# DeltaNet and soft MoE on one core: unscaled keys, block transposes on VectorE, and 24 chunk slots with work eight chunks ahead

## The chip, the core and the metric

The kernel runs on one core of one Trainium2 chip. Five engines of that core work side by side, each through its own instructions in order: TensorE (PE in the profile, its weight loads PEld), VectorE (DVE), ScalarE (ACT), GpSimd (POOL) and SyncE (SP), which here only issues DMAs. TensorE reads SBUF and writes PSUM; the other engines move results back. The metric is the device time of one execution in microseconds (us), lower is better.

## The reference

An attention block with the delta rule feeds a mixture of experts with soft slots. Four batches times eight heads are 32 independent sequences of 768 tokens with head size 48; everything is float32.

```python
k_n = k / (np.linalg.norm(k, axis=-1, keepdims=True) + 1e-06)
for t in range(S):
    kt, vt, bt = (k_n[:, :, t], v[:, :, t], beta[:, :, t, None])
    y[:, :, t] = np.einsum('bhd,bhde->bhe', q[:, :, t], state)
    v_old = np.einsum('bhde,bhd->bhe', state, kt)
    state = state + bt[:, :, :, None] * np.einsum('bhd,bhe->bhde', kt, vt - v_old)
...
logits = x @ phi                                  # x: (3072, 384), 32 slots
d = softmax of logits over the 3072 tokens
slot_input = d.T @ x
slot_out = per expert e: relu(slot_input[e] @ w1[e]) @ w2[e]
c = softmax of logits over the 32 slots
return c @ slot_out
```

`x` is the attention output, with the eight heads of a token side by side.

## The kernel before, in words

**Chunks and groups.** The 768 tokens are cut into 24 chunks of 32. Within a chunk the recurrence is solved as a triangular system, so that only the state S (48x48 for each of the 32 sequences) passes from chunk to chunk. Four chunks are a group; there are six groups. On the 128 partitions lie four heads (index `h`) times 32 tokens; the other eight of the 32 (batch, head) pairs (`U = 8`) lie side by side on the free axis.

**Norms (L155 to L180), per group.** POOL squares the keys (L163), DVE adds them up (L164) and takes the root with one correction step (L168 to L174, the square root itself on ACT), and POOL multiplies the keys by the reciprocal (L177).

**Preparation of a chunk (`prep`, L182).** TensorE transposes K and Q (L193), ACT copies the result to KQ (L196), TensorE multiplies K with K and with Q (L208); ACT copies the K-K products to `Lc` (L212) and DVE masks the others into `AT` with `tri` (L213). `pt`, the PSUM tile of these steps and of the routing, has two buffers, so TensorE cannot be more than two tiles ahead of the copies.

**Inversion of a group (`invert`, L218).** The 128 triangular systems of a group (32 sequences times four chunks) are inverted at once, one system per partition. For that `Lc` has to be regrouped: four DMAs write it to DRAM (`ld`, L228), one reads it back (`lb`, L229), and POOL multiplies by beta (L230). Then come 31 eliminations of two DVE operations each (L242 and L245). POOL multiplies by beta again (L249), a DMA writes the inverse to DRAM (`td`, L252), and per chunk four DMAs bring its part back (`TT`, L262).

**A chunk (`chunk`, L272)** is a chain: psR (L282), R = V - psR on DVE (L287), psW with the inverse (L293), U on DVE (L296), psS (L303), then the state S, half copied by ACT (L315) and half by DVE (L313), and the next chunk's psR needs S. psY (L282 and L320) and its copy Y (L322) hang beside the chain.

**Routing of a group (`route`, L330)**: transposes of Y (L340), logits (L349), both softmaxes with a running maximum, and the sums over tokens (L414).

**After the six groups** come the experts (L553, L577) and the output (L603 to L610). Two of the eight w1 are loaded early, the other weights once the attention's buffers are free.

**Order.** The kernel hands out steps: `Fill` puts a quarter of a slot's steps between the stages of a chunk, `merge` interleaves lists. In group n the first two chunks carry the preparation of group n+1, the last two its inversion and the routing of group n-1. The Tile framework then fixes each engine's order; every instruction waits in its place on its engine.

Of the kernel before, what the change touches and what calls it, by code (L numbers as in the profile page):

```python
# [16 lines left out]
def kernel(  # L17
# [20 lines left out]

    nc = tc.nc
    P = 128  # L40
# [19 lines left out]
    dp = ctx.enter_context(tc.tile_pool(name="dp", bufs=2, space=bass.MemoryType.DRAM))  # L60
# [14 lines left out]
    def load(src, dst, n, eng):  # L75
        for c in range(GC):
            for h in range(4):
                s0 = (n * GC + c) * C
                eng.dma_start(
                    out=dst[C * h:C * h + C, c, :, 0:D],  # L80
                    in_=src.rearrange("b (g h) s d -> h s (b g) d", h=4)[h, s0:s0 + C])

    def load_k(n, eng=nc.sync):
        load(k, Ks[n % 3], n, eng)

    def load_q(n, eng=nc.sync):
        load(q, Qs, n, eng)

    def load_v(n, eng=nc.sync):
        Vt[n] = io.tile([P, GC, U, D], F32, name="V", tag="V")  # L90
        load(v, Vt[n], n, eng)

    for t in Ks + [Qs]:
        nc.gpsimd.memset(t[:, :, :, D:DP], 0.0)

    bb = cpool.tile([P, NG, C], F32, name="bb")
    load_k(0)
    load_q(0, nc.scalar)
    for h in range(4):
        for c in range(GC):  # L100
            p0 = C * h + U * c
            nc.scalar.dma_start(
                out=bb[p0:p0 + U],
                in_=beta.rearrange("b (g h) (n c t) -> h c (b g) n t", h=4, c=GC, t=C)[h, c])
    load_v(0)
    phi = cpool.tile([GD, 4, NSL], F32, name="phi")
    for g in range(G):
        nc.scalar.dma_start(
            out=phi[g * D:(g + 1) * D],
            in_=moe_phi[g * 4 * D:(g + 1) * 4 * D].rearrange("(h d) s -> d h s", h=4))  # L110


    ident = cpool.tile([P, P], F32, name="ident")
    make_identity(nc, ident)
# [15 lines left out]
    TTs = [wk.tile([P, U, C], F32, name=f"TT{i}", bufs=1) for i in range(2)]  # L130
# [22 lines left out]
    KQ, AT, Lc, TTb = {}, {}, {}, {}  # L153

    def norm(n):  # L155
        Kf = Ks[n % 3].rearrange("p c u d -> p (c u) d")
        ssq = small.tile([P, GC * U], F32, name="ssq", tag="ssq")
        nrm = small.tile([P, GC * U], F32, name="nrm", tag="nrm")
        rn = small.tile([P, GC * U], F32, name="rn", tag="rn")

        def squares():
            sq = wk.tile([P, GC * U, D], F32, name="sq", tag="sq", bufs=1)
            nc.gpsimd.tensor_tensor(sq, Kf[:, :, 0:D], Kf[:, :, 0:D], op=ALU.mult)  # L163
            nc.vector.tensor_reduce(ssq, sq, axis=AX.X, op=ALU.add)  # L164

        def root():

            nc.vector.tensor_scalar(ssq, ssq, 1e-30, None, op0=ALU.max)  # L168
            nc.scalar.activation(nrm, ssq, ACT.Sqrt)
            nc.vector.reciprocal(rn, nrm)  # L170
            nc.vector.tensor_tensor(rn, rn, ssq, op=ALU.mult)
            nc.vector.tensor_tensor(nrm, nrm, rn, op=ALU.add)
            nc.vector.tensor_scalar(nrm, nrm, 0.5, 1e-6, op0=ALU.mult, op1=ALU.add)
            nc.vector.reciprocal(rn, nrm)  # L174

        def scale():
            nc.gpsimd.tensor_tensor(Kf[:, :, 0:D], Kf[:, :, 0:D],  # L177
                                    rn.unsqueeze(2).broadcast_to([P, GC * U, D]), op=ALU.mult)

        return [squares, root, scale]  # L180

    def prep(n, c):  # L182

        cc = n * GC + c

        def transposes(bh):
            if bh == 0:
                KQ[cc] = wk.tile([P, B, 2, P], F32, name="KQ", tag="KQ", bufs=2 * GC - 1)
            tp = pt([P, 2, 2, P])
            for i in range(2):  # L190
                b = 2 * bh + i
                for a, src in enumerate((Ks[n % 3], Qs)):
                    nc.tensor.transpose(  # L193
                        tp[:, i, a, :],
                        src[:, c, b * G:(b + 1) * G, :].rearrange("p g d -> p (g d)"), ident)
            nc.scalar.activation(KQ[cc][:, 2 * bh:2 * bh + 2], tp, ACT.Copy)  # L196

        def products():
            AT[cc] = wk.tile([P, G, B, C], F32, name="AT", tag="AT", bufs=2 * GC - 1)
            if c == 0:  # L200
                Lc[n] = wk.tile([P, GC, B, G, C], F32, name="Lc", tag="Lc", bufs=1)
            pg = [pt([P, B, 2, C]) for _ in range(G)]
            for b in range(B):
                for h in range(4):
                    for g in range(G):
# [4 lines left out]
                                         start=True, stop=True, skip_group_check=True)  # L210
            for g in range(G):
                nc.scalar.activation(Lc[n][:, c, :, g, :], pg[g][:, :, 0, :], ACT.Copy)  # L212
# [5 lines left out]
    def invert(n):  # L218
# [3 lines left out]
        def spread():  # L222
            lb = st["lb"] = wk.tile([P, C, C], F32, name="lb", tag="lb", bufs=1)
            lc = Lc.pop(n).rearrange("p c b g t -> p (c b g) t")
            ld = dp.tile([P, C, C], F32, name="ld", tag="ld")
            for h in range(4):
# [3 lines left out]
            nc.gpsimd.tensor_tensor(lb, lb, bb[:, n].unsqueeze(2).broadcast_to([P, C, C]),  # L230
                                    op=ALU.mult)
# [4 lines left out]

# [402 lines left out]
```

## Time and profile before

| | us |
|---|---|
| runs (three) | 605.12, 606.75, 613.19; median 606.75 |
| profiled execution, its own time | 610.76 |
| its span (first to last instruction) | 609.0 |
| PE busy | 333.6 (55% of the span) |
| DVE busy | 253.1 (42%) |
| ACT busy | 113.5 (19%) |
| POOL busy | 71.2 (12%) |
| mean granted TensorE clock | 0.698 of full speed |

The time lies 1.76 us above the span: what passes before the first and after the last instruction. PEclk is the clock that TensorE was granted, 1.00 being full speed. In a row of the windows view stand the stretch, its length, then busy time and count of PE, PEld, DVE, ACT and POOL, then PEclk, the share of the DMA engines and GB/s. In a row of the groups view stand line, engine, operation, tiles, shape and count, then busy time in all and mean ns of one, then the idle time of the engine before them and what ended it. In a row of the waits view: who waited for whom, us in all, times, the longest. In the timeline: start, length, what.

### The profile page before, as it was taken

What the parts mean: (1) busy time and instruction counts of PE and PEld (TensorE: products, weight loads), DVE (VectorE), ACT (ScalarE), POOL (GpSimd) and SP (SyncE); (2) the same over time, 40 slices, a digit from 0 to 9 for tenths busy, and PEclk for the clock granted to TensorE, in tenths of its full rate; (3) what the DMA queues carried; (4) which work ended last, traced back from release to release, by engine and by line L of the source; (5) the groups of instructions that cost most, each with busy time, mean ns of one, the idle gap of its engine ahead of it and who ended that gap; (6) DMA issues with size and microseconds to landing.
All of it is one profiled execution on the core that took longest, in us unless ns stands there. A gap on an engine that the chain in (4) does not pass through costs nothing.

```text
span 609.0 us, 20685 instructions
## 1 busy us (share of the span) xinstructions
PE 333.6 (55%) x9387; PEld 252.6 (41%) x9387; DVE 253.1 (42%) x661; ACT 113.5 (19%) x232; POOL 71.2 (12%) x62
## 2 busy tenths in 40 slices
PE   0360274550189730697702877405987528769675
PEld 0250153540167520576601665304766417553224
DVE  2214951129812369223297123693246722130013
ACT  0230130110033310223200323102343001211003
POOL 4203110011210110400303001103001010000000
PEclk9995556675557975568755588855689565869975
DMA  6406017562034510235300445102230024497918
GB/s 118 80 15 133 8 37 216 110 119 46 1 85 79 118 29 0 67 67 111 62 0 6 83 74 114 30 0 58 35 74 3 1 55 119 177 427 278 430 42 311
DMA packets 138296, 58.12 MB, mean 95 GB/s; under 512 B 131552, under 2 KB 134624, under 8 KB 136160
## 3 DMA queue, kind: packets, MB, share of 16 engines
q1 hardware_dynamic: 132544, 55.87, 34.6%
q10 hardware_dynamic: 5664, 0.94, 0.9%
q8 instruction: 73, 1.20, 0.8%
q14 instruction: 15, 0.12, 0.1%
HBM read 45.76 MB, written 11.01 MB: 93 GB/s over the span
## 4 chain that ended last, share of the span: by engine, by line
PE 44%; DVE 26%; DMA 12%; issue 5%; ACT 5%; SPq 4%; POOL 3%; ACTq 0%; DVEq 0%
DVE pr L242 9%; DVE tt L245 9%; PE pt L193 7%; PE psW L293 5%; PE pt L208 4%; PE pt L414 4%; PE psR L282 4%; PE psY L320 3%; PE psS L303 3%; DMA w2t<-in_moe_w_dram 3%; PE psY L282 3%; PE pt L340 3%; PE pso L577 2%; DMA TT<-td 2%; DMA Qs<-in_q_dram 2%
## 5 line engine op out<-in xcount | busy, mean ns | idle before, releaser
L193 PE MATMUL pt<-ident,Ks 128*128 128x128 f32 x96 | 40.4, 422 | 172.4 <-POOL Ks L177 137.5
L193 PEld LDWEIGHTS pt<-ident,Ks 128*128 128x128 f32 x96 | 20.1, 210 | 177.8 <-POOL Ks L177 163.6
L242 DVE TENSOR_TENSOR pr<-tt,lb 128x31 f32<-128x31 f32 (+15 forms) x186 | 78.0, 419 | 18.5 <-POOL lb L230 13.4
L245 DVE TENSOR_TENSOR tt<-tt,pr 128x31 f32<-128x31 f32 (+15 forms) x186 | 65.9, 355 | 5.5
L293 PE MATMUL psW<-R,TT 32*32 32x48 f32 x1536 | 37.5, 232 | 27.1 <-DMA TT<-td 25.1
L208 PE MATMUL pt<-KQ 48*32 48x64 f32 x1536 | 41.5, 287 | 6.0 <-issue 4.1
L293 PEld LDWEIGHTS psW<-R,TT 32*32 32x32 f32 x1536 | 29.4, 126 | 36.9 <-DMA TT<-td 19.6
L296 DVE COPY U<-psW 128x384 f32<-128x384 f32 x24 | 13.4, 557 | 74.9 <-PE psW L293 74.9
L196 ACT ACTIVATE KQ<-pt 128x512 f32<-128x512 f32 x48 | 28.4, 597 | 78.7 <-PE pt L193 78.7
L313 DVE COPY S<-psS 48x768 f32<-48x768 f32 x23 | 22.1, 960 | 46.0 <-ACT S L315 46.0
L193 PE MATMUL pt<-ident,Qs 128*128 128x128 f32 x96 | 38.8, 407 | 0.0
L315 ACT ACTIVATE S<-psS 48x768 f32<-48x768 f32 x23 | 18.5, 804 | 103.6 <-PE psS L303 103.2
L282 PE MATMUL psR<-S,KQ 128*32 128x96 f32 x768 | 31.8, 303 | 8.5 <-DVE S L313 6.0
L213 DVE TENSOR_TENSOR AT<-pt,tri 128x128 f32<-128x128 f32 x48 | 12.0, 286 | 58.6 <-ACT Lc L212 58.6
L208 PEld LDWEIGHTS pt<-KQ 48*32 48x32 f32 x1536 | 28.8, 140 | 18.1 <-ACT KQ L196 10.1
L320 PE MATMUL psY<-U,AT 32*32 32x48 f32 x1536 | 29.4, 233 | 4.9 <-issue 4.1
L177 POOL TENSOR_TENSOR Ks<-Ks,rn 128x1536 f32<-128x1536 f32 x6 | 16.6, 2770 | 123.7 <-DVE pr L242 88.8
L282 PE MATMUL psY<-S,KQ 128*32 128x96 f32 x768 | 29.9, 297 | 1.7 <-issue 1.7
L282 PEld LDWEIGHTS psR<-S,KQ 128*32 128x32 f32 x768 | 23.4, 135 | 14.4 <-DVE S L313 7.9
L303 PE MATMUL psS<-U,Ks 32*48 32x48 f32 x1472 | 22.7, 242 | 11.3 <-DVE U L296 8.7
L414 PE MATMUL pt<-Y,dr 32*32 32x97 f32 x768 | 26.1, 308 | 4.0 <-ACT dr L407 4.0
L320 PEld LDWEIGHTS psY<-U,AT 32*32 32x32 f32 x1536 | 24.7, 128 | 8.1 <-issue 5.9
(118 smaller groups left out, 438.8 us busy)
## 6 DMA issues: line engine op xcount, KB each, us to landing
w1t<-in_moe_w_dram SPq DMA_DIRECT2D x8, 1536.0 KB
w2t<-in_moe_w_dram SPq DMA_DIRECT2D x8, 1536.0 KB
Ks<-in_k_dram SPq DMA_DIRECT2D x96, 48.0 KB
V<-in_v_dram SPq DMA_DIRECT2D x96, 48.0 KB
out_dram<-ob SPq DMA_DIRECT2D x24, 192.0 KB
Qs<-in_q_dram SPq DMA_DIRECT2D x80, 48.0 KB
ld<-Lc SPq DMA_DIRECT2D x24, 128.0 KB
lb<-ld SPq DMA_DIRECT2D x6, 512.0 KB
```

Of the source, the lines that this page charges most:

```text
L193: nc.tensor.transpose(tp[:, i, a, :], src[:, c, b * G:(b + 1) * G, :].rearrange("p g d -> p (g d)"), ident)
L196: nc.scalar.activation(KQ[cc][:, 2 * bh:2 * bh + 2], tp, ACT.Copy)
L208: nc.tensor.matmul(pg[g][rh, b], lhsT=KQ[cc][r, b, 0, rh], rhs=KQ[cc][r, b, :, rh], start=True, stop=True, skip_group_check=True)
L242: nc.vector.tensor_tensor(prv, tt[:, 0:m, j:j + 1].broadcast_to([P, m, w]), lb[:, j, j + 1:C].unsqueeze(1).broadcast_to([P, m, w]), op=ALU ...
L245: nc.vector.tensor_tensor(tt[:, 0:m, j + 1:C], tt[:, 0:m, j + 1:C], prv, op=ALU.subtract)
L282: nc.tensor.matmul(dst[hs[h], b].rearrange("p g d -> p (g d)"), lhsT=kq[:, b, a, hs[h]], rhs=old[:, h, b, :], start=(b == 0), stop=False, ...
L293: nc.tensor.matmul(pw[hs[h], u], lhsT=T[hs[h], u], rhs=R[hs[h], u], start=(u == 0), stop=True, skip_group_check=True)
L303: nc.tensor.matmul(psS[DP * g:DP * g + D, h, b * D:(b + 1) * D], lhsT=K[hs[h], c, b * G + g, 0:D], rhs=Ut[hs[h], b * G + g], start=(cc == ...
L313: nc.vector.tensor_copy(dst, src)
L315: nc.scalar.activation(dst, src, ACT.Copy)
L320: nc.tensor.matmul(py[hs[h], b, g], lhsT=at[hs[h], g, b], rhs=Ut[hs[h], b * G + g], start=False, stop=True, skip_group_check=True)
L414: nc.tensor.matmul(pa[r], lhsT=st["dr"][r, c, b, :], rhs=Yn[r, c, b, 0:GD + 1], start=(b == 0), stop=(b == B - 1), skip_group_check=True)
```

## The change

**Unscaled keys.** The norm of a key now comes from the diagonal of the K-K products (`norms`), so the steps on whole key tiles are gone (squares, their sum, the scaling). With nm the norm plus 1e-6, the weight of a token becomes `gm` = beta / nm^2, and V is multiplied by nm (`scale_v`, one POOL operation of 128x384 per chunk); keys stay as loaded.

**Transposes on DVE.** `Lc` is written so that a 32x32 block transpose on DVE regroups it (`spread`); after the eliminations, which now run over the rows of `tt`, a second one turns the inverse back (`back`). The DRAM tiles and their DMAs are gone. U is copied by ACT instead of DVE, with two buffers, as has R.

**24 slots.** Loads are per chunk. A slot x runs chunk x, prepares chunk x+8, does a quarter of the inversion of the next group and a quarter of the last group's routing, loads K and Q twelve ahead and V six ahead. Slots -8 to -1 have no chunk. Beta and phi are loaded from POOL instead of ACT.

```diff
-    Ks = [io.tile([P, GC, U, DP], F32, name=f"Ks{i}", bufs=1) for i in range(3)]
-    Qs = io.tile([P, GC, U, DP], F32, name="Qs", bufs=1)
+    LEAD, AHEAD = 8, 12
+    NK, NQ = AHEAD + 1, AHEAD - LEAD + 1
+    Ks = [io.tile([P, U, DP], F32, name=f"K{i}", bufs=1) for i in range(NK)]
+    Qs = [io.tile([P, U, DP], F32, name=f"Q{i}", bufs=1) for i in range(NQ)]
...
     for h in range(4):
         for c in range(GC):
             p0 = C * h + U * c
-            nc.scalar.dma_start(
+            nc.gpsimd.dma_start(
                 out=bb[p0:p0 + U],
...
-    def norm(n):
...
-            nc.gpsimd.tensor_tensor(sq, Kf[:, :, 0:D], Kf[:, :, 0:D], op=ALU.mult)
-            nc.vector.tensor_reduce(ssq, sq, axis=AX.X, op=ALU.add)
...
-            nc.gpsimd.tensor_tensor(Kf[:, :, 0:D], Kf[:, :, 0:D],
-                                    rn.unsqueeze(2).broadcast_to([P, GC * U, D]), op=ALU.mult)
...
+            by = Lc[n].rearrange("p t (c b g) -> p c g b t", c=GC, b=B)
             for g in range(G):
-                nc.scalar.activation(Lc[n][:, c, :, g, :], pg[g][:, :, 0, :], ACT.Copy)
+                nc.scalar.activation(by[:, c, g], pg[g][:, :, 0, :], ACT.Copy)
...
         def spread():
             lb = st["lb"] = wk.tile([P, C, C], F32, name="lb", tag="lb", bufs=1)
-            for h in range(4):
-                r = slice(C * h, C * h + C)
-                nc.sync.dma_start(out=ld[r].rearrange("u s t -> s u t"), in_=lc[r])
-            nc.sync.dma_start(out=lb, in_=ld)
-            nc.gpsimd.tensor_tensor(lb, lb, bb[:, n].unsqueeze(2).broadcast_to([P, C, C]),
-                                    op=ALU.mult)
+            nc.vector.transpose(lb.rearrange("p t s -> p (t s)"),
+                                Lc.pop(n).rearrange("p t c -> p (t c)"))
...
+        def norms():
...
+            dg = st["lb"].rearrange("p t s -> p (t s)")[:, 0:C * C:C + 1]
+            nc.vector.tensor_scalar(ssq, dg, 1e-30, None, op0=ALU.max)
+            nc.scalar.activation(nrm, ssq, ACT.Sqrt)
...
+            nc.vector.tensor_tensor(gm, rn, rn, op=ALU.mult)
+            nc.vector.tensor_tensor(gm, gm, bb[:, n], op=ALU.mult)
+            nc.gpsimd.tensor_tensor(st["lb"], st["lb"],
+                                    gm.unsqueeze(2).broadcast_to([P, C, C]), op=ALU.mult)
+            nT[n] = small.tile([P, C], F32, name="nT", tag="nT")
+            nc.vector.transpose(nT[n], nrm)
...
-            TTb[n] = dp.tile([P, C, C], F32, name="td", tag="td")
-            nc.sync.dma_start(out=TTb[n], in_=st["tt"])
+        def back():
+            TT[n] = wk.tile([P, C, C], F32, name="TT", tag="TT")
+            nc.vector.transpose(TT[n].rearrange("p c i -> p i c"), st["tt"])
...
+    def scale_v(cc):
         n, c = divmod(cc, GC)
+        nc.gpsimd.tensor_tensor(
+            Vt[cc], Vt[cc], nT[n][:, c * U:(c + 1) * U].unsqueeze(2).broadcast_to([P, U, D]),
+            op=ALU.mult)
...
-        nc.vector.tensor_copy(Ut, pw)
+        nc.scalar.activation(Ut, pw, ACT.Copy)
...
+    for x in range(-LEAD, NCH):
+        n, c = divmod(x, GC)
+        if x + AHEAD < NCH:
+            load_k(x + AHEAD)
+            load_q(x + AHEAD)
+        if 0 <= x + 6 < NCH:
+            load_v(x + 6)
...
+        if c == 0:
+            inv = invert(n + 1) if 0 <= n + 1 < NG else []
+        if 0 <= x + 2 < NCH:
+            scale_v(x + 2)
+        steps = merge(prep(x + LEAD) if x + LEAD < NCH else [], quarter(inv, c),
+                      quarter(routing, c))
+        if x < 0:
+            drain(steps)
+            continue
+        fill = Fill(steps)
+        chunk(x, Ys[n % 2], fill)
+        fill(last=True)
+        if c == GC - 1:
+            routing = route(n, Ys[n % 2])
```

**Place one: POOL at the start.** Before, after the pads of the key tiles, POOL prepares `bdm`, from which DVE makes the mask `tri`:

```order
L94 MEMSET Ks_78 128x32x16
L94 MEMSET Ks_79 128x32x16
L94 MEMSET Ks_80 128x32x16
L94 MEMSET Qs 128x32x16
masks.py:197 MEMSET ident 128x128
L116 MEMSET hm 128x4
L123 MEMSET bdm 128x128
masks.py:199 ISA
masks.py:199 AFFINE_SELECT ident<-ident 128x128
L117 AFFINE_SELECT hm<-hm 128x4
L124 AFFINE_SELECT bdm<-bdm 128x128
```

Now, on the same engine:

```order
masks.py:197 MEMSET ident 128x128
L113 DMA bb<-in_beta_dram 8x6x32
masks.py:199 ISA
masks.py:199 AFFINE_SELECT ident<-ident 128x128
L113 DMA bb<-in_beta_dram 8x6x32 x15
L118 DMA phi<-in_moe_phi_dram 48x4x32 x2
L124 MEMSET hm 128x4
L131 MEMSET bdm 128x128
L125 AFFINE_SELECT hm<-hm 128x4
```

The 18 DMAs of beta and phi stand on POOL ahead of `bdm`, and so ahead of the first mask that DVE applies.

**Place two: PE in a loaded slot.** Before, from the second to the third chunk of the second group, with routing beside it:

```order
L303 MATMUL psS<-U,Ks_79 48x48 x32
L320 MATMUL psY<-U,AT 32x48 x32
L340 MATMUL pt<-ident,Y_581 96x128 x5
L282 MATMUL psR<-S_173,KQ 32x96 x16
L282 MATMUL psY<-S_173,KQ 32x96 x16
L293 MATMUL psW<-R,TT_170 32x48 x32
```

Now, in chunk 10 of 0 to 23 (K_79 holds the keys of chunk 16, which is prepared meanwhile):

```order
L278 MATMUL psR<-S_180,KQ 32x96 x16
L278 MATMUL psY<-S_180,KQ 32x96 x13
L173 MATMUL pt<-ident,Q_90 128x128
L173 MATMUL pt<-ident,K_79 128x128
L173 MATMUL pt<-ident,Q_90 128x128 x2
L173 MATMUL pt<-ident,K_79 128x128
L173 MATMUL pt<-ident,Q_90 128x128
L278 MATMUL psY<-S_180,KQ 32x96 x3
L336 MATMUL pt<-ident,Y_188 96x128 x4
L188 MATMUL pt<-KQ 32x64 x32
L336 MATMUL pt<-ident,Y_188 96x128 x4
L289 MATMUL psW<-R,TT 32x48 x32
```

Between psR and psW there now stand six of the eight transposes and all products of another chunk.

**Place three: DVE in the same slot.** Before, the eliminations of a group end in one block and the chunk's own operations follow:

```order
L242 TENSOR_TENSOR pr<-tt,lb 128x31
L245 TENSOR_TENSOR tt<-tt,pr 128x31
L213 TENSOR_TENSOR AT<-pt,tri 128x128 x6
L296 COPY U<-psW 128x384
L313 COPY S_175<-psS 48x16x48
L287 TENSOR_TENSOR R<-V,psR 128x384
```

Now, around the R of the same slot:

```order
L243 TENSOR_TENSOR tt<-tt,pr 128x21x11
L195 TENSOR_TENSOR AT<-pt,tri 128x128 x2
L240 TENSOR_TENSOR pr<-tt,lb 128x240
L243 TENSOR_TENSOR tt<-tt,pr 128x20x12
L240 TENSOR_TENSOR pr<-tt,lb 128x247
L283 TENSOR_TENSOR R<-V,psR 128x384
L243 TENSOR_TENSOR tt<-tt,pr 128x19x13
```

R stands behind the masks AT of the prepared chunk and behind three eliminations; in the whole list the 62 operations of an inversion lie almost wholly in two of a group's four slots, with AT, R and S strewn among them.

More of the change, by code (lines that the diff above doesn't have):

```diff
@@ L128 @@
     nc.vector.tensor_reduce(tri, bdm.rearrange("p h t -> p t h"), axis=AX.X, op=ALU.add)
-    TTs = [wk.tile([P, U, C], F32, name=f"TT{i}", bufs=1) for i in range(2)]
     psS = psp.tile([P, 4, 512], F32, name="psS")
@@ L149, in load_w2, with prep @@
         nc.sync.dma_start(out=w2t[e], in_=moe_w2[e].rearrange("(p t) d -> p t d", t=NFC))
[L153 to L184 removed]
+    KQ, AT, Lc, TT, nT = {}, {}, {}, {}, {}
+    def prep(cc):
+        n, c = divmod(cc, GC)
         def transposes(bh):
             if bh == 0:
[L188 removed]
+                KQ[cc] = wk.tile([P, B, 2, P], F32, name="KQ", tag="KQ", bufs=LEAD + 1)
             tp = pt([P, 2, 2, P])
```

140 lines of the change are left out of this document (58 added, 82 removed).

## The prediction

> **What bounds the kernel now.** I read the busy time by stretches first, with borders at the first transposes of each group (POOL's scaled keys release them), then who waits for whom, then the chain. Columns of the stretches: PE, PEld, DVE, ACT, POOL busy (instructions), granted clock, DMA share, GB/s.
>
> ```profile
> 161.60:244.20 82.60, 46.49 (x1524) 37.68 (x1524) 40.73 (x109) 18.15 (x35) 11.22 (x8) 0.69 0.29 57
> 228.00:232.00 4.00, 0.00 (x0) 0.00 (x0) 3.69 (x10) 0.00 (x0) 0.00 (x0) 0.50 0.00 0
> 497.80:526.00 28.20, 22.28 (x874) 18.34 (x878) 6.77 (x10) 3.88 (x6) 0.00 (x0) 0.64 0.29 78
> 526.00:545.30 19.30, 13.48 (x254) 10.47 (x240) 3.65 (x18) 4.45 (x10) 0.83 (x4) 0.65 1.00 408
> PE pt L193 <- POOL Ks L177: 137.5, 5, 29.8
> PE psW L293 <- DMA TT<-td: 25.1, 4, 11.6
> 110.92 1.92 PE psW L293 x64
> 525.61 0.93 PE psY L320 x64
> ```
>
> No engine is full. A middle group takes 82.6 us, of which TensorE works 46.5 and VectorE 40.7, one after the other: in the second row DVE eliminates and PE does nothing. PE's waits for the scaled keys, 137.5 us in five, are that block seen from PE. Three parts make up the span: a head to the first psW at 110.9, the chunks to the last psY at 526.5, and 82.5 us of last routing, experts and output. The four chunks of the last group, with neither preparation nor inversion, take 28.2 us.
>
> **The head.** Rows: SP's and ACT's first DMAs, the first and the fourth chunk's transposes, and the root of the norms from its first to its last operation.
>
> ```profile
> 0.80 10.03 SPq L79 DMA_DIRECT2D Ks<-in_k_dram  x16
> 11.57 6.36 ACTq L102 DMA_DIRECT2D bb<-in_beta_dram  x16
> 24.86 1.95 PE pt L193 x8
> 39.55 0.33 PE L193 MATMUL pt<-ident,Ks 128*128 128x128 f32 x1 [0.68 <-DVE AT L213]
> 17.86 0.18 DVE L168 TENSOR_SCALAR ssq<-ssq 128x32 f32<-128x32 f32 x1
> 21.53 0.35 DVE L174 RECIPROCAL rn<-nrm 128x32 f32<-128x32 f32 x1
> L242 DVE TENSOR_TENSOR pr<-tt,lb 128x31 f32<-128x31 f32 (+15 forms) x186 | 78.0, 419 | 18.5 <-POOL lb L230 13.4
> L245 DVE TENSOR_TENSOR tt<-tt,pr 128x31 f32<-128x31 f32 (+15 forms) x186 | 65.9, 355 | 5.5
> L230 POOL TENSOR_TENSOR lb<-lb,bb 128x1024 f32<-128x1024 f32 x6 | 11.5, 1911 | 68.6 <-DMA lb<-ld 41.0 <-DMA Ks<-in_k_dram 27.6
> L249 POOL TENSOR_TENSOR tt<-tt,bb 128x1024 f32<-128x1024 f32 x6 | 14.1, 2352 | 35.1 <-DVE tt L245 35.1
> L164 DVE TENSOR_REDUCE ssq<-sq 128x32 f32<-128x1536 f32 x6 | 10.5, 1747 | 11.4 <-POOL sq L163 11.4
> L287 DVE TENSOR_TENSOR R<-V,psR 128x384 f32<-128x384 f32 x24 | 13.3, 554 | 33.7 <-PE psR L282 31.0 <-DMA Qs<-in_q_dram 2.5
> L213 DVE TENSOR_TENSOR AT<-pt,tri 128x128 f32<-128x128 f32 x48 | 12.0, 286 | 58.6 <-ACT Lc L212 58.6
> ```
>
> Chunk 0 needs four K loads from SP at 0.63 us each (10.03 / 16): issued by 3.3, there near 6, where before all 16 and the norms had to pass and PE began at 24.9. But the masks AT need `tri`, and POOL now issues 18 DMAs before it prepares `bdm`. No row has a DMA issued by POOL; the nearest are ACT's own issue of beta (0.40) and SP's of keys (0.63): 7.2 to 11.3 us. I take 11.3 and some 3.5 for what else stands there: `tri` near 15. [...]
>
> With two `pt` buffers the second chunk waits for the first one's AT. The rows at 24.86 and 39.55 are three chunks apart, 4.9 each, so `Lc` of the first group is whole near 15 + 3 x 4.9 + 0.6 = 30. (Its last keys are issued by SP as numbers 21 to 24, so by 16; not late.) Then, in series:
>
> - block transpose of 128x1024. No row has one. The reduction of 1536 elements in 1747 ns gives 1.2 us for 1024; POOL's pass over 1024 in 2352 is the dear end. I take 1.2; at the dear end twelve transposes cost 14 us more.
> - the root chain, 17.86 to 21.88 = 4.0, with two more small products: 4.5; POOL's lb 1.9.
> - 62 eliminations: (78.0 + 65.9) / 6 = 24.0. They change their order of axes, not their elements. Four AT among them: 1.1.
> - POOL's tt 2.4, the transpose back 1.2, R 0.55.
>
> Sum 37, so R of chunk 0 near 67 and psW with it, against 110.9: 44 us gained, with the ld/lb and td/TT trips and the norms of group 1 out of the way. The range is 60 to 75.
>
> **A slot.** First the serial chain when PE runs cold, in one stretch of the trace.
>
> ```profile
> 443.55 1.51 PE L282 MATMUL psR<-S,KQ 128*32 128x96 f32 x32 [1.71 <-DVE AT L213]
> 444.79 1.56 PE L282 MATMUL psY<-S,KQ 128*32 128x96 f32 x32
> 436.35 0.83 PE L282 MATMUL psY<-S,KQ 128*32 128x96 f32 x32
> 417.52 1.87 PE L208 MATMUL pt<-KQ 48*32 48x64 f32 x64
> 419.81 0.49 DVE L213 TENSOR_TENSOR AT<-pt,tri 128x128 f32<-128x128 f32 x2 [3.96 <-ACT Lc L212]
> 508.88 1.56 PE psW L293 x64
> L322 ACT ACTIVATE Y<-psY 128x384 f32<-128x384 f32 x24 | 11.8, 490 | 18.9 <-PE psY L320 18.7
> 431.35 1.08 PE L303 MATMUL psS<-U,Ks 32*48 32x48 f32 x64 [0.27 <-DVE U L296]
> L315 ACT ACTIVATE S<-psS 48x768 f32<-48x768 f32 x23 | 18.5, 804 | 103.6 <-PE psS L303 103.2
> L313 DVE COPY S<-psS 48x768 f32<-48x768 f32 x23 | 22.1, 960 | 46.0 <-ACT S L315 46.0
> ```
>
> In the new order six of the eight transposes and all products of another chunk stand on PE between psR and psW, and R stands on DVE behind their AT. So a loaded slot is: psR 1.51, psY 1.56, transposes 1.95 x 6 / 8 = 1.46, products 1.87, copy and AT 0.9 (419.39 to 420.30), R 0.55, psW 1.56, U 0.49 (as Y, the same shape on ACT; no wait is added, U's old place on DVE is free), psS 1.08, S 0.80 + 0.96, and ten handoffs of about 0.06: 13.3 us. At full clock psY is 0.83 instead of 1.56; applying 0.6 to the PE terms (9.0) leaves 9.7. At the middle group's clock of 0.69, between them: 11.6. Routing adds PE time: 13.48 / 4 = 3.4 a slot by the last routing's row, half of it in waits; and some 0.8 for eliminations that stand ahead of R or S. A slot light in eliminations thus takes 14 us, without routing 12.5.
>
> Two of a group's four slots are heavy: each holds half the eliminations on DVE (12.0, and 1.0 for gaps), AT 0.57, R 0.55, S 0.96, a POOL pass that the next elimination or the transpose waits for (1.9 or 2.4), a share of norms or routing (1.0): 18 minus what overlaps the pass, 17. Here DVE is the bound. POOL also scales V, 2.77 x 384 / 1536 = 0.7 us per chunk:
>
> ```profile
> 412.78 2.78 POOL L177 TENSOR_TENSOR Ks<-Ks,rn 128x1536 f32<-128x1536 f32 x1 [29.72 <-DVE pr L242]
> 412.98 2.63 DVE L242 TENSOR_TENSOR pr<-tt,lb 128x31 f32<-128x31 f32 x1
> ```
>
> The smallest elimination, which starts while POOL multiplies, ends when POOL does. So the scaling of V holds DVE; its 0.7 is in the 17 of heavy slots and falls into waits in light ones. The old scaling, 2.8 a group, is what it replaces.
>
> The sum over slots: the first four, without routing, 2 x 17 + 2 x 12.5 = 59. Three groups of 2 x 17 + 2 x 14 = 62: 186. Slots 16 to 19 have no preparation, so bare chunks of 28.2 / 4 = 7.1 and routing stand beside DVE's work: 24 eliminations, 6 for R and S, 7 for norms and transposes, 4.3 of POOL passes, 3.7 routing, that is 45. The last four: 28.2, routing of group 4 half hidden, and the rest of the last inversion: 36 to the last psY. Together 326, against 415.6 before.
>
> **The tail** is unchanged code: 82.5. The weights' buffers come free with the last chunk, as before.
>
> Span 67 + 326 + 82.5 = 475.5, time 477.3 against this execution's 610.76; as the median is 606.75, scaled by it: 474.
>
> Loads cost nothing: 12 a chunk at 0.63 are 7.6 us of SP in a slot of 12 or more; if a slot fell under 7.6, SP would bound. What comes late next is R, behind AT and eliminations.
>
> **The rivals.**
>
> *The clock stays full.* The rows:
>
> ```profile
> 176.00:180.00 4.00, 4.00 (x128) 3.21 (x127) 0.80 (x3) 0.89 (x3) 0.00 (x0) 0.50 0.44 76
> 192.00:196.00 4.00, 4.00 (x101) 3.34 (x100) 0.96 (x1) 2.29 (x4) 0.00 (x0) 0.50 0.32 54
> 200.00:204.00 4.00, 2.24 (x101) 1.82 (x99) 0.96 (x1) 1.68 (x4) 0.00 (x0) 1.00 0.36 72
> ```
>
> PE can be full at 0.50 and half idle at 1.00. Were it 1.00 throughout, light slots would take 1.9 less, the last eight 1.5 less each: 475 - 8 x 1.9 - 12 = 448. [...] The two full stretches at 0.50 speak against. 13%.
>
> *DVE packs without waiting.* A loaded group's DVE work, with POOL's passes and holds, is 24 + 2 + 2.3 AT + 2.2 R + 3.8 S + 7 + 3.7 + 4.3 + 2.8 = 52, 13 a slot; with a head of 62 that gives 62 + 48 + 3 x 52 + 40 + 28 + 82 = 416. It needs the masks never to wait for PE. 5%.
>
> *R and S come late in every slot.* If half of DVE's side work were added to the chain everywhere, loaded slots would take about 20: 72 + 4 x 18 + 12 x 20 + 48 + 36 + 82.5 = 550. For it: DVE takes its list strictly in order. Against: R and S are spread among the eliminations, each of them 0.4 us. 9%.
>
> *Slower.* One mechanism: nothing overlaps. PE cold in the chain (13.3), routing all on it (3.4), and DVE's other work (52 - 8.3) / 4 = 11 a slot behind it, makes 27.7 in a routed slot, 24 without: 75 + 4 x 24 + 12 x 27.7 + 68 + 36 + 82.5 = 690. It decides for slower once routed slots take 23.3 us (same formula, other slots shortened with them). Before, PE and DVE did alternate like that, but because of a wait for the whole inversion, which eight chunks of lead remove. 2%; 3% for ending within 2%.
>
> **How the numbers follow.** Forecast, 68%: 430 to 520, from the head's 60 to 75, heavy slots of 15.5 to 19 and light ones of 11.5 to 16; likeliest 474. With the full clock inside it, 420 to 520 leaves out the packed case, the late one and the two at the end, 19%. Faster by over 2%, about what these runs can tell: 0.95; within 0.03; slower 0.02.
>
> **What would show it.** First psW near 67, PE waiting for AT in the first 15 to 22 us. PE never idle for 30 us; its waits short, for R and S. In every group two slots with DVE over 90% busy and two paced by PE. No DMA of ld, lb, td or TT. Last psY to end still 82 to 83. I am wrong if a block transpose takes over 3 us, if TensorE stands at 0.50 all through, or if R waits for eliminations in light slots.

## The result and the profile after

| | before | changed |
|---|---|---|
| median of four runs, us | 608.88 (605.12 to 613.19) | 488.61 (485.43 to 491.42) |
| ratio | | 0.802, 95% interval 0.794 to 0.810 |
| profiled execution: time, span | 610.76, 609.0 | 491.42, 489.7 |
| mean granted clock | 0.698 | 0.729 |
| first psW (start) | 93.72 | 63.51 |
| copy of the last psY (start) | 526.56 | 403.62 |
| from there to the end | 82.4 | 86.1 |

The forecast was 474, with a range of 430 to 520 (420 to 520 with the full clock in it). Ratios leave out runs over 1.5% above the fastest of the same kernel. Of the 119.3 us that the span lost, the head gave 30.2 and the chunks 92.7; the tail took 3.7 back. The prediction put the end of the head before at 110.92, but that row is the second chunk's psW. The first chunk's begins here (in brackets, how long the engine stood idle before it and for what):

```profile
93.72 0.70 PE L293 MATMUL psW<-R,TT 32*32 32x48 f32 x4 [4.83 <-DMA TT<-td]
```

The stretches of the changed kernel, columns as in the prediction: the first four slots from psW on, the next three groups of four, slots 16 to 19 (all further borders at the copy of U) and the last four to the end of the last Y.

```profile
63.51:127.89 64.38, 39.78 (x1376) 33.17 (x1376) 34.26 (x89) 14.23 (x29) 8.25 (x9) 0.63 0.27 46
127.89:190.50 62.61, 44.91 (x1428) 35.82 (x1428) 36.32 (x100) 19.28 (x38) 8.47 (x9) 0.69 0.25 43
190.50:256.80 66.30, 51.04 (x1524) 40.04 (x1524) 38.49 (x106) 20.86 (x40) 8.51 (x9) 0.69 0.23 39
256.80:321.63 64.83, 49.42 (x1524) 39.20 (x1524) 37.90 (x106) 20.65 (x41) 7.37 (x7) 0.71 0.10 18
321.63:377.73 56.10, 39.34 (x1455) 31.35 (x1456) 40.88 (x115) 18.07 (x35) 10.03 (x10) 0.91 0.11 35
377.73:404.10 26.37, 20.77 (x992) 17.78 (x994) 5.66 (x10) 7.19 (x13) 0.00 (x0) 0.86 0.14 47
```

A group that took 82.6 us takes 62.6 to 66.3, with PE busy 45 to 51 of them: PE and DVE now overlap. But neither is full, and the waits show what is missing (first, as above, who waited for whom, us in all, times, the longest):

```profile
PEld psW L289 <- DVE R L283: 49.3, 17, 10.4
PE psW L289 <- DVE R L283: 45.5, 15, 10.1
PEld pt L173 <- DVE AT L195: 20.2, 6, 9.2
```

The five waits for a whole inversion (137.5 us) are gone. In their place PE waits 15 times for R, once in the head (10.1 us) and 14 times in the slots (35.4). The timeline of one slot (13; these are some of its rows) shows what stands ahead of R:

```profile
263.60 0.87 PE L278 MATMUL psR<-S,KQ 128*32 128x96 f32 x32
264.29 0.85 PE L278 MATMUL psY<-S,KQ 128*32 128x96 f32 x32
265.66 1.08 ACT L176 ACTIVATE KQ<-pt 128x512 f32<-128x512 f32 x2 [1.44 <-PE pt L173]
267.11 1.21 PE L188 MATMUL pt<-KQ 48*32 48x64 f32 x64
268.33 0.60 ACT L194 ACTIVATE Lc<-pt 128x128 f32<-128x128 f32 x2 [1.59 <-PE pt L188]
268.75 0.51 DVE L195 TENSOR_TENSOR AT<-pt,tri 128x128 f32<-128x128 f32 x2 [1.25 <-ACT Lc L194]
269.17 1.23 DVE L207 STREAM_TRANSPOSE lb<-Lc 128x1024 f32<-128x1024 f32 x1
270.94 0.55 DVE L283 TENSOR_TENSOR R<-V,psR 128x384 f32<-128x384 f32 x1
271.55 1.50 PE L289 MATMUL psW<-R,TT 32*32 32x48 f32 x64 [0.94 <-DVE R L283]
```

psR is whole at 264.47; R, which needs nothing else but V, starts 6.47 us later. It stands behind the masks of another chunk, which wait for that chunk's transposes, copies and products, and then behind the block transpose and a sum of the routing. In the kernel before, R followed psR after 0.06 us in nearly every chunk. Here the delay is 6.2 to 11.6 us in fourteen of slots 1 to 17 and 6.8 on the mean of these seventeen (psR's last end to R's start in the timeline). What stands ahead of R differs. In the slots without eliminations it is the masks, as here. In the others DVE eliminates meanwhile: in slots 2, 6, 10 and 14 eliminations and the masks stand ahead of R, in 3 and 7 the end of the inversion with its second block transpose (11.6 and 11.2 us), in 11 and 15 eliminations and routing without any mask. The stretch from psR to R in slot 11 and in slot 13:

```profile
231.09:237.72 6.63, 4.39 (x136) 3.29 (x127) 6.15 (x22) 3.45 (x7) 0.00 (x0) 0.96 0.35 59
264.47:270.94 6.47, 5.00 (x167) 3.87 (x158) 2.18 (x6) 2.97 (x5) 0.00 (x0) 0.86 0.01 3
```

DVE is busy for 6.15 us of the first and for 2.18 of the second.

The head, from the same view: the mask, the first and the fourth AT, the block transposes, the first elimination, POOL's last pass, and R of chunk 0.

```profile
13.26 0.37 DVE L136 TENSOR_REDUCE tri<-bdm 128x32 f32<-128x128 f32 x1
13.74 0.49 DVE L195 TENSOR_TENSOR AT<-pt,tri 128x128 f32<-128x128 f32 x2
26.65 0.51 DVE L195 TENSOR_TENSOR AT<-pt,tri 128x128 f32<-128x128 f32 x2 [4.14 <-ACT Lc L194]
27.08 1.23 DVE L207 STREAM_TRANSPOSE lb<-Lc 128x1024 f32<-128x1024 f32 x1
32.89 0.19 DVE L240 TENSOR_TENSOR pr<-tt,lb 128x31 f32<-128x31 f32 x1 [2.03 <-POOL lb L230]
56.93 1.91 POOL L247 TENSOR_TENSOR tt<-tt,gm 128x1024 f32<-128x1024 f32 x1 [24.07 <-DVE tt L243]
58.87 1.91 DVE L253 STREAM_TRANSPOSE TT<-tt 128x1024 f32<-128x1024 f32 x1 [2.09 <-POOL tt L247]
62.90 0.55 DVE L283 TENSOR_TENSOR R<-V,psR 128x384 f32<-128x384 f32 x1 [1.80 <-POOL V L259]
```

### The profile page after: what moved, and what is told of

Its sections match the earlier page's. It is cut to its first block, busy times and chain, and to the rows that moved or that the text cites. A ratio compares the mean times of both kernels' runs of the same rounds, so it can differ in the third digit from the quotient of the medians.

```text
span 489.7 us, 20564 instructions
## 1 busy us (share of the span) xinstructions
PE 334.7 (68%) x9387; PEld 248.3 (51%) x9387; DVE 245.1 (50%) x679; ACT 128.9 (26%) x257; POOL 63.6 (13%) x88
## 4 chain that ended last, share of the span: by engine, by line
DVE 27%; issue 25%; PE 19%; SPq 10%; DMA 10%; POOL 5%; ACT 3%; DVEq 0%; POOLq 0%; ACTq 0%
DVE pr L240 9%; SPq L80 9%; DVE tt L243 9%; DMA w2t<-in_moe_w_dram 4%; PE pso L567 3%; DVE S L309 3%; PE psR L278 2%; PE pt L410 2%; DMA w1t<-in_moe_w_dram 2%; PE psY L278 2%; POOL lb L230 2%; DMA Q<-in_q_dram 2%; DVE TT L253 2%; PE ph L543 1%; DMA out_dram<-ob 1%
## 5 line engine op out<-in xcount | busy, mean ns | idle before, releaser
L240 DVE TENSOR_TENSOR pr<-tt,lb 128x31 f32<-128x31 f32 (+15 forms) x186 | 68.0, 365 | 17.7 <-POOL lb L230 12.2
L243 DVE TENSOR_TENSOR tt<-tt,pr 128x31 f32<-128x31 f32 (+15 forms) x186 | 66.3, 357 | 5.7
L173 PE MATMUL pt<-ident,K 128*128 128x128 f32 x96 | 36.0, 396 | 24.1 <-DVE AT L195 18.7
L316 PE MATMUL psY<-U,AT 32*32 32x48 f32 x1536 | 39.0, 256 | 3.2 <-issue 3.1
L188 PE MATMUL pt<-KQ 48*32 48x64 f32 x1536 | 33.5, 246 | 6.2 <-ACT KQ L176 2.6
L299 PE MATMUL psS<-U,K 32*48 32x48 f32 x1472 | 25.3, 261 | 14.5 <-ACT U L292 11.6
L278 PEld LDWEIGHTS psR<-S,KQ 128*32 128x32 f32 x768 | 23.7, 145 | 22.4 <-DVE S L309 18.9
L173 PEld LDWEIGHTS pt<-ident,K 128*128 128x128 f32 x96 | 17.3, 186 | 30.7 <-DVE AT L195 20.2
L292 ACT ACTIVATE U<-psW 128x384 f32<-128x384 f32 x24 | 11.8, 490 | 75.6 <-PE psW L289 75.6
L299 PEld LDWEIGHTS psS<-U,K 32*48 32x48 f32 x1472 | 20.4, 155 | 20.7 <-ACT U L292 15.7
L230 POOL TENSOR_TENSOR lb<-lb,gm 128x1024 f32<-128x1024 f32 x6 | 11.5, 1911 | 141.0 <-DVE gm L229 141.0
L173 PE MATMUL pt<-ident,Q 128*128 128x128 f32 x96 | 29.7, 364 | 0.0
```

The source lines that it names most:

```text
L173: nc.tensor.transpose(tp[:, i, a, :], src[:, b * G:(b + 1) * G, :].rearrange("p g d -> p (g d)"), ident)
L188: nc.tensor.matmul(pg[g][rh, b], lhsT=KQ[cc][r, b, 0, rh], rhs=KQ[cc][r, b, :, rh], start=True, stop=True, skip_group_check=True)
L240: nc.vector.tensor_tensor(prv, tt[:, j, 0:m].unsqueeze(1).broadcast_to([P, w, m]), lb[:, j, j + 1:C].unsqueeze(2).broadcast_to([P, w, m]), ...
L243: nc.vector.tensor_tensor(tt[:, j + 1:C, 0:m], tt[:, j + 1:C, 0:m], prv, op=ALU.subtract)
L278: nc.tensor.matmul(dst[hs[h], b].rearrange("p g d -> p (g d)"), lhsT=kq[:, b, a, hs[h]], rhs=old[:, h, b, :], start=(b == 0), stop=False, ...
L299: nc.tensor.matmul(psS[DP * g:DP * g + D, h, b * D:(b + 1) * D], lhsT=K[hs[h], b * G + g, 0:D], rhs=Ut[hs[h], b * G + g], start=(cc == 0 a ...
```

## The experiments

Three questions: which part of the change pays, what the late R costs, and what the new work on POOL costs. All ratios and times are against the same kernel before, 607.95 to 609.62 us in these comparisons.

### Which part pays: the trips, the plan, the keys

**Trips through DRAM put back**, all else as changed but the order of axes in the eliminations, which goes back with them (136.3 us in all against 134.3).

```
-            nc.vector.transpose(lb..., Lc.pop(n)...)
+            for h in range(4): nc.sync.dma_start(out=ld[r]..., in_=lc[r])
+            nc.sync.dma_start(out=lb, in_=ld)
...
-            nc.vector.transpose(TT[n]..., st["tt"])
+            nc.sync.dma_start(out=td, in_=st["tt"])
+            for h in range(4): nc.sync.dma_start(out=TT[n][C * h:C * h + C], in_=td[...])
```

> The changed kernel with the two block transposes of a group undone: Lc goes to DRAM and back as before, and so does the inverse, with four DMAs per group on the way back; all else (slots, unscaled keys, loads) as changed. Before, the first pass through DRAM lay between the fourth chunk's products and POOL's scaling. Theory (the lead of eight chunks is what pays in the groups, the transposes only in the head): the head grows by 20 to 30 us, each of the five other groups by 0 to 8, time 510 to 550. Rival (the transposes pay in every group, since the trip stands ahead of the eliminations and ahead of the next group's first psW): over 20 us in each group, time above 590.

558.83 us (ratio 0.920, 0.911 to 0.929), between the theory's range and the rival's. First psW at 99.5, so 36 us of head, more than I gave. The groups of slots 4 to 15 grew too, to 75.6, 78.3 and 66.9 us from 62.6, 66.3 and 64.8 (U to U): 12 to 13 us in two of them, where the theory gave 0 to 8. So the transposes pay in the groups as well. The waits of this kernel say how:

```profile
PE psW L297 <- DMA TT<-td: 112.5, 20, 32.9
```

In the first chunk of each of groups 1 to 3 psW stood 32 to 38 us after its R: the inverse arrived late, since the trip stands ahead of the eliminations and behind them.

**The old plan with the new operations**: a lead of one group, the inversion in the last two chunks.

```
-    LEAD, AHEAD = 8, 12
+    LEAD, AHEAD = 4, 8
...
+        if c < 2:
+            steps = prep(first) + prep(first + 1) if inv else []
+        elif c == 2:
+            steps = merge(inv[:cut_i], routing[:cut_r])
+        else:
+            steps = merge(inv[cut_i:], routing[cut_r:])
```

> The changed kernel's operations (unscaled keys, block transposes, loads per chunk, U on ACT) in the old plan: a lead of one group, the first two chunks of a group prepare two chunks each, the last two take the inversion and the routing. Theory (the lead pays): TensorE stands still for some 20 us of eliminations in every group again, a group takes 75 to 80 us against 62 to 66, the time is 540 to 580. Rival (the operations pay, the plan does not): 485 to 505.

527.59 us (0.868, 0.859 to 0.878): below the theory's range and far above the rival's. The head is the changed kernel's (psW at 63.4). The row of a middle group, and the wait that costs:

```profile
203.40:271.03 67.63, 43.81 (x1525) 35.04 (x1526) 37.25 (x106) 20.05 (x40) 8.62 (x9) 0.75 0.22 38
PE psW L289 <- DVE TT L253: 78.5, 6, 31.5
```

So without the lead the first psW of groups 1 to 5 comes 19 to 31 us after its R. TensorE fills part of that with other work: of the 78.5 us of its waits 31.5 lie in the head, and in four of the five groups it stands still for 11 to 12 us, not for 20. The three middle groups take 66.1, 67.6 and 67.6 us, only 1.3 to 3.5 more than the same groups of the changed kernel. Outside the head the lead removes 47.0 us of waiting for the inverse and puts 35.4 of waiting for R in its place. By these two runs the transposes are worth 70 us with the new plan, and the plan 39 with the transposes. Of these 39 some 10 lie in each of three places: in the first group (72.4 us from U to U against 62.8), in the last with an inversion beside it (65.5 against 56.1), and in the tail (96.2 against 86.1), where PE waits 12.2 us for w1 and w2 instead of 6.6; the middle groups hold most of the rest, 7.6.

**Scaled keys put back**, with the norms taken from the keys as before.

```
+            nc.gpsimd.tensor_tensor(sq, Kc[:, :, 0:D], Kc[:, :, 0:D], op=ALU.mult)
+            nc.vector.tensor_reduce(ssq[:, c * U:(c + 1) * U], sq, axis=AX.X, op=ALU.add)
...
-            nc.vector.tensor_tensor(gm, gm, bb[:, n], op=ALU.mult)
+            gm = st["gm"] = bb[:, n]
...
-            scale_v(x + 2)
+            norm((x + LEAD) // GC)
```

> The changed kernel with the keys scaled again: per group POOL squares four key tiles, VectorE adds up (0.44 us each), takes the root, POOL multiplies the four tiles by the reciprocal, all ahead of the group's preparation; gm is beta alone and V is not scaled. Slots and block transposes as changed. Theory (it costs where it is in series): the head grows by 8 to 12 us, a loaded group by 1 to 5 for 4 us more on VectorE, time 500 to 520. Rival (unscaled keys are a main part of the gain): above 530. Rival (they pay nothing): 485 to 493.

510.86 us (0.841, 0.833 to 0.848), as the theory had it: first psW at 74.1, 10.6 us later. The unscaled keys are worth 22 us, half of them in the head (two runs).

### What the late R costs

**The changed kernel with its written order kept** on TensorE and VectorE, not one operation altered. The framework had let the preparation slip: on PE chunk 10 stood beside the preparation of chunk 16, where the text says 18.

```
+    man.enter_context(tc.manual_schedule(engines={mybir.EngineType.PE, mybir.EngineType.DVE}))
     for x in range(-LEAD, NCH):
```

> The changed kernel with not one operation altered or moved in its text: TensorE and VectorE only keep the order in which it is written, in place of the one the framework lays out. The first quarter of the other work then stands between psY and psW, R stands directly behind psR. Theory (the late R comes from the order laid out, which lets the preparation run two slots late and puts it between psR and R): R within 1 us of psR in most slots, loaded slots 14 to 14.5, time 440 to 455. Rival (what gained was moving the first quarter behind U): 470 to 490.

442.27 us (0.727, 0.723 to 0.731), 46 less than the changed kernel, with the same instructions. The same two steps in slot 11 of this kernel:

```profile
203.32 1.51 PE L278 MATMUL psR<-S,KQ 128*32 128x96 f32 x32
204.95 0.55 DVE L283 TENSOR_TENSOR R<-V,psR 128x384 f32<-128x384 f32 x1 [0.53 <-PE psR L278]
```

```profile
109.82:164.90 55.08, 38.63 (x1527) 31.02 (x1525) 38.31 (x103) 20.39 (x40) 8.87 (x9) 0.88 0.29 50
164.90:219.94 55.04, 39.26 (x1527) 31.99 (x1525) 38.83 (x106) 20.60 (x42) 8.87 (x9) 0.84 0.24 42
219.94:276.37 56.43, 38.85 (x1520) 31.56 (x1517) 38.00 (x103) 20.11 (x40) 9.34 (x9) 0.82 0.10 19
```

R is late by 1.5 us on the mean of slots 1 to 17 (6.8 in the changed kernel), a group takes 55 to 56 us, 13.8 to 14.1 a slot (14 to 14.5 expected). "Within 1 us in most slots" held in only seven of the seventeen; four more stay under 1.3, the others wait up to 5 us behind eliminations, routing and, in slot 4, the second block transpose. The same 1525 or so matmuls take 39 us of PE instead of 49 to 51, at a granted clock of 0.82 to 0.88 instead of 0.69 to 0.71: about what a group lost, PE's own busy time lost. What the clock did by itself and what the order did can't be parted here. That the four runs of the changed kernel had clocks of 0.729, 0.752, 0.753 and 0.795 and times of 491.4, 488.7, 485.4 and 488.5 us speaks against the clock alone, but none of them comes near 0.85. Nor was R's place changed alone: the order of two engines was.

**The same, with the first quarter of the other work moved behind U.**

```
-        fill()
         pw = ps.tile([P, U, D], F32, name="psW", tag="psRW")
...
         nc.scalar.activation(Ut, pw, ACT.Copy)
         fill()
+        fill()
```

> TensorE and VectorE keep the order in which the kernel is written, and the first quarter of the other work comes after U instead of after psR. So R no longer stands behind the masks AT of the prepared chunk, psW follows psY directly, the preparation really runs eight chunks ahead, and the eliminations lie evenly over the four slots. In the changed kernel R starts 6.4 to 7.4 us after its psR in a loaded slot, and such a slot takes 16.3 us with TensorE busy 12 to 13 of them. Theory (the chain psR, transposes, products, AT, R, psW sets the slot): R follows psR within 0.5 us, loaded slots fall to TensorE's own 12.5 to 13.5, the time falls to 425 to 450 us. Rival (TensorE at its granted clock sets the slot, R waits for nothing that matters): slots stay above 15.5 and the time at 475 to 495. Rival (VectorE's sum sets it): slots near 13 as well, but VectorE busy over 90% in every slot.

440.44 us (0.724, 0.718 to 0.731): in the theory's range, its slots at 13.5 to 14.2, a little above it, and R within 0.5 us in only six of slots 1 to 17. Beside the run above (1.8 us apart) it says that the place of this quarter is worth nothing that these runs can tell. The rival of TensorE as the bound falls, and so does VectorE's sum: DVE is busy for 57 to 80% of each of slots 1 to 17.

**The same as the last run, but only TensorE's order kept**; VectorE's list is the framework's again.

> As the kernel with both orders fixed, but only TensorE keeps the written order; VectorE's list is again laid out by the framework, with the eliminations in two of four slots. Theory: the light slots gain as there, the heavy ones stay near 15 to 17, so about half of the gain: 445 to 470 us. Rival (the order on TensorE is all that matters): the same time as there within 5 us. Rival (the order on VectorE is all that matters): 480 to 495, as the changed kernel.

452.69 us (0.745, 0.737 to 0.753; two runs), in the theory's range. R is late in no slot by more than 1.3 us, but DVE's half of S now starts 1.6 to 7 us after the end of ACT's in most loaded slots, behind eliminations. So PE's order alone carries 36 of the 48 us, and adding DVE's written order, which spreads the eliminations, the other 12. DVE's order alone was not run.

### The new work on POOL

**Masks ahead of the 18 DMAs.**

```
+    hm = ...; bdm = ...; tri = ...
     bb = cpool.tile([P, NG, C], F32, name="bb")
     for h in range(4):
         for c in range(GC): nc.gpsimd.dma_start(out=bb[p0:p0 + U], ...)
...
-    hm = ...; bdm = ...; tri = ...
```

> The changed kernel with the masks bdm and tri prepared ahead of POOL's 18 DMAs of beta and phi. In the changed kernel tri is ready at 13.6 us and the first AT starts at 13.74, while its products were copied at 10.7. Theory (the DMAs on POOL hold the first mask, and the four preparations of the head follow one another through AT): first AT near 10.8, the fourth AT 3 us earlier (23.7 against 26.7), the first psW near 60.5 against 63.5. Rival (the head is paced by the loads of keys or by the fixed chain after them): first AT earlier, but the fourth one and the first psW move by under 1 us.

First AT at 10.93, the fourth at 23.71, first psW at 60.26, and 483.72 us (0.796, 0.789 to 0.803), 4.9 less. The theory holds to a quarter of a microsecond in each place. These places give 3.2 us; the rest of the 4.9 lies within the spread of the runs (482.06 and 485.39, against 485.43 to 491.42).

**V not scaled.**

```
-        if 0 <= x + 2 < NCH:
-            scale_v(x + 2)
```

> The changed kernel without the scaling of V by the norm (24 operations of POOL, 0.83 us each); V is taken as loaded, everything else is kept, so the output lacks that factor. Theory as in the prediction (POOL's product holds VectorE, which counts only in slots that VectorE bounds, and R of two chunks waits for it): 3 to 9 us less. Rival (the hold counts in every slot): 15 to 20 us less. Rival (it counts nowhere, the waits lie elsewhere): within 2 us.

475.22 us (0.783, 0.779 to 0.787): 13.4 less, above the theory's 3 to 9 and below the rival's 15. The timeline of the changed kernel shows the hold on DVE, the same operation beside POOL and (in the head, above) without it:

```profile
209.58 1.61 POOL L259 TENSOR_TENSOR V<-V,nT 128x384 f32<-128x384 f32 x2
209.65 0.80 DVE L240 TENSOR_TENSOR pr<-tt,lb 128x31 f32<-128x31 f32 x1 [2.03 <-POOL lb L230]
210.49 0.77 DVE L243 TENSOR_TENSOR tt<-tt,pr 128x31 f32<-128x31 f32 x1
```

0.80 us against 0.19. DVE's two operations start while POOL's two run and end at 211.26, POOL's at 211.19; what ties them together is not shown. Over all eliminations the sums are 134.3 us with the scaling and 127.5 without, 6.8 of the 13.4. R waits for V twice in the changed kernel, 1.8 us in the head and 1.6 in slot 3: 3.4 more, which is gone with the scaling. And the framework also laid out another order: in chunk 7 R came ahead of the second block transpose, and its delay fell from 11.2 to 5.9.

To see whether the rest is POOL's list, the scaling was put four chunks ahead.

> The changed kernel with the scaling of V four chunks ahead, behind the slot's other work, instead of two ahead and in front of it. Leaving the scaling out had gained 13 us, not 3 to 9. In the changed kernel eliminations beside a product of POOL ran over by 7 us in all against the same shapes elsewhere. Theory (about half of the 13 is the hold on VectorE, which stays; the other half is R and the eliminations waiting behind POOL's list): 4 to 7 us less than the changed kernel, 481 to 485. Rival (all of it is the hold): 487 to 490. Rival (all of it is waiting in POOL's list): 474 to 478.

489.68 us (0.803, 0.799 to 0.807). The number lies in the rival's range, yet it decides nothing: the framework set the operations back to nearly the same places (two of them at 210.41, where the changed kernel has them at 209.58), so little was moved. The order had to be fixed first:

> The kernel that keeps the written order, without the scaling of V (the output lacks that factor). Without it the framework had also laid out another order in the changed kernel, so that its 13 us mix two things; here the lists of TensorE and VectorE are the same with and without it. The eliminations take 137.8 us with the scaling beside them against 127.5 in the run without it: 10.3 us of hold. Theory (VectorE is near its bound in this order, so the hold counts almost in full): 7 to 12 us less than the same kernel with it. Rival (the hold falls into waits): within 3 us.

> The kernel that keeps the written order once more, on the same chip as the run without the scaling of V, to compare the two: 440 to 444 us as before. Were it over 3 us away from 442, differences between chips would have to be taken off the other comparisons.

430.77 us without, 441.07 with, 10.3 apart by the medians of six runs each (8.8 without the two longest of the runs with it). The groups of the two kernels, without and with:

```profile
L243 DVE TENSOR_TENSOR tt<-tt,pr 128x31 f32<-128x31 f32 (+15 forms) x186 | 64.2, 345 | 6.4
L240 DVE TENSOR_TENSOR pr<-tt,lb 128x31 f32<-128x31 f32 (+15 forms) x186 | 63.1, 339 | 15.8 <-POOL lb L230 11.5
```

```profile
L243 DVE TENSOR_TENSOR tt<-tt,pr 128x31 f32<-128x31 f32 (+15 forms) x186 | 69.5, 374 | 6.4
L240 DVE TENSOR_TENSOR pr<-tt,lb 128x31 f32<-128x31 f32 (+15 forms) x186 | 68.3, 367 | 15.8 <-POOL lb L230 11.5
```

10.5 us longer eliminations (137.8 against 127.3), 9 to 10 us of time: with the order fixed, the hold counts nearly in full. The rival that it falls into waits is out for this order; for the framework's order, how much of the 6.8 us of hold counts among the 13.4 stays open.

### A version from these findings

Fixed order, psS directly behind U and four transposes, both halves of S on ACT, finer steps of routing, masks first, and in the tail two loads in another order:

```
         if e == 5:
+            load_w2(4, wp2, 6)
+            load_w2(5, wp2, 6)
...
-                if g:
-                    nc.vector.tensor_copy(dst, src)
-                else:
-                    nc.scalar.activation(dst, src, ACT.Copy)
+                nc.scalar.activation(dst, src, ACT.Copy)
```

> Built on the kernel with both orders fixed: only a quarter of the other work between psW and psS, both halves of the state copied by ACT so that S no longer stands in VectorE's list, the routing's steps cut finer, the inversion ends earlier in the fourth slot of a group, masks ahead of POOL's DMAs, and two w2 are issued ahead of the two w1 that wait for buffers, since DMA stood still for 8 us there. Theory (with R free, the late psS and S are next): loaded slots 11.5 to 12.5 against 14.1, the tail 6 to 8 us shorter, time 395 to 415. Rival (VectorE's sum of about 10 a slot and its strict order bound it already): slots 13 to 14, the time 425 to 435.

419.16 us (413.09 to 422.21), the shortest of all, between the theory's range and the rival's; its runs lie too far apart for an interval. The tail is 76.9 us (339.50 to 416.4) against 86.1, 9.2 less: the theory's 6 to 8 and a little more. In the changed kernel DMA stood nearly still behind two w1 that waited for their buffers, and PE then waited for the last w2 in the chain:

```profile
428.62:433.62 5.00, 5.00 (x41) 1.63 (x43) 0.00 (x0) 0.79 (x4) 0.00 (x0) 1.00 0.13 52
443.41 17.82 DMA w2t<-in_moe_w_dram
```

The slots miss their mark: 13.0 to 13.8, as the rival had it. The place in its slot 12:

```profile
215.29 0.61 ACT L194 ACTIVATE Lc<-pt 128x128 f32<-128x128 f32 x2 [0.92 <-PE pt L188]
217.98 0.48 DVE L195 TENSOR_TENSOR AT<-pt,tri 128x128 f32<-128x128 f32 x2
218.32 0.84 PE L338 MATMUL pt<-ident,Y 128*96 128x128 f32 x4 [3.06 <-DVE AT L195]
```

AT could start at 215.9, where the copies end, stands behind eliminations, and PE, which needs its buffer, waits 3.06 us. So what comes late after R is, in this slot, AT, again on DVE.

## Why the prediction was right, and where its steps were off

**The total** was right to 3%: 474 forecast, 488.6 measured, and the sign and size with it (120 us less, 133 forecast). That it came so near is in part luck, since errors cancel below. Against the forecast span of 475.5 the measured 489.7 is 14.2 longer: head -3.5, chunks +14.1, tail +3.6.

**The head**: right, 63.5 for 67, with errors both ways. `tri` was ready at 13.6 (15 forecast), which the masks put first confirm as the right term; a preparation took 4.3 us, (26.65 - 13.74) / 3, not 4.9, so `Lc` was whole at 26.8, not 30. The 16 DMAs of beta took 0.56 us each in POOL's list (1.46 to 10.75, with one other operation among them), between the 0.40 and 0.63 of ACT's and SP's rows. Two ends of ranges, 22 us for PE's wait for AT at the start and 75 for the head, were estimates that no run bears out: PE's first wait for AT ended at 14.09, and the first psW came at 63.5. The first block transpose cost 1.23 as forecast, the second 1.91, for which I had taken 1.2. The root chain took 2.5 (28.34 to 30.86), not 4.5. The eliminations, with their gaps and two masks among them, took 24.04 (32.89 to 56.93; 24.0 forecast, and 1.1 for four masks). A term was missing: R waited 1.8 us for V, behind POOL's memset of the next `tt`. The gain of 44 us was misread: the head before ended at 93.72, so 30 were gained, and the chunks before took 432.8, not 415.6. The forecast time does not rest on either, since its terms are summed for the new kernel.

**The first four slots** took 64.4, not 59. The largest is slot 3 with 19.6 for 17: R stood behind the end of the inversion, the second block transpose, the masks and V.

**The loaded groups**: the sum was near, the split wrong. 62 forecast, 62.6, 66.3 and 64.8 measured. The chain of a light slot was the right mechanism there: six transposes, products, copy and AT between psR and R, named there as "R stands on DVE behind their AT" (slot 13 above). That R came on time and the group fell to 55 us with the order fixed supports it. In light slots no elimination stood between psR and R, so that sign of being wrong did not appear. But the step "two heavy slots of 17, two light ones of 14" failed: it fits slots 5 to 8 (13.3, 18.3, 19.7, 11.3, each from the U before to its own), while slots 9 to 16 take 15.4 to 17.6 each, with DVE over 90% busy in one of four rather than two, and in none of slots 5 to 8. The light ones among 9 to 16 take 16.2 to 16.9 instead of 14. Ahead of slots 12 and 16 DVE's half of S starts 1.9 to 2.0 us after ACT's half ends, behind eliminations; ahead of 9 and 13 it starts at once (0.03), and what they miss stays open.

**V's scaling** was mis-sized: 0.7 us in eight heavy slots, 5.6 in all, where the changed kernel lost 13.4 to it and, with the order fixed, 9 to 10.

**The last two groups**: two errors that cancel, which was luck. 45 and 36 forecast, 56.1 and 26.4 measured, 81 against 82.5. The step that failed is that slots 16 to 19 hold only DVE's sum. The preparation runs six chunks ahead, not eight, so the last `Lc` was whole only in slot 17 (near 332); DVE worked 4.66 us from chunk 16's U to chunk 17's, and the inversion then ran to 376.1, which the first psW of the last group (the last row here) needs:

```profile
321.63:336.69 15.06, 11.50 (x439) 9.05 (x440) 4.66 (x12) 6.43 (x12) 0.00 (x0) 1.00 0.09 18
374.14 1.90 DVE L253 STREAM_TRANSPOSE TT<-tt 128x1024 f32<-128x1024 f32 x1
376.10 1.50 PE L289 MATMUL psW<-R,TT 32*32 32x48 f32 x64 [1.44 <-DVE TT L253]
```

That a place of the order showed chunk 16 beside chunk 10 was before my eyes; I did not carry it into the sum.

**The tail**: "unchanged code, 82.5" was 3.6 short, and why is not shown. It is the same chain; its first product of the experts came 23.7 us after the last Y's copy (427.36) against 21.8 (548.38), and the wait for the last w2 ended 57.7 after it against 55.7.

**The rivals.** The full clock didn't come (0.729). The DVE-bound case, 52 us a group, was not reached by the change; the fixed order comes near it in time with 55, but with DVE busy for 38.3 of them. "R and S late in every slot" did happen for R in fourteen of seventeen slots, but loaded slots took some 16 us, not 20: most of the delay of a light slot was already in its sum. "Nothing overlaps" did not happen.

## What to carry to other kernels

Where the work ahead of a serial chain is made early, the wait for it need not vanish. Here it moved to R, a small operation of the chain that shares an engine with that work, because the framework's order put it behind. Compare the laid-out order with the written one, by the distance between a producer's end and its consumer's start in each period, before counting on a lead. And with the order free, an experiment that removes an operation may move others, as R in chunk 7; fix the order first.

## What was not expected of the hardware

- Two block transposes of the same 128x1024 float32 differ: 1.23 us for the one whose output is written in order, 1.92 for the one whose output is written with a stride (the inverse turned to chunk order). No run changes the stride alone.
- POOL's product of 128x384 (0.83 us) stretches the smallest elimination from 0.19 to 0.80 us; 24 of them cost 9 to 10 us of a 441 us kernel.
- The granted clock went with the order of the same matmuls: 0.69 to 0.71 in groups with a late R, 0.82 to 0.88 with the order fixed, and PE's busy time for them fell from 49 to 51 us to 39.
